# Attention with a recurrent state and a mixture of experts: the attention's preparation in an explicit order, with merged transfers and more k buffers

## The chip, the cores and the metric

The kernel runs on one core of a Trainium2 chip. The metric is the device time in microseconds of one launch. The profile is of one further execution on the same core, taken by the hardware profiler; its times are counted from the first instruction.

## The reference, cut to what matters

Attention over 4 x 8 heads of 768 tokens with 40 values each keeps a 40 x 40 state per head, which decays, loses a rank-one term and gains one at each token. Its output is the input of a router and of 8 experts, of which each token uses two.

```python
for t in range(S):
    y[:, :, t] = einsum('bhd,bhde->bhe', rt, state)
    Sa = einsum('bhde,bhe->bhd', state, at)
    state = state * wt[:, :, None, :] - einsum('bhd,bhe->bhde', Sa, bt) + einsum('bhd,bhe->bhde', vt, kt)
x = y.transpose(0, 2, 1, 3).reshape(B*S, H*D)
noisy_logits = x @ w_gate + log1p(exp(x @ w_noise)) * noise
# the two best experts of each token, weighted by a softmax of their logits:
#   out += weight * (relu(x @ w1[e]) @ w2[e])
```

## The kernel before, in words

The attention is computed in chunks of 64 tokens. A chunk of one pair of batch entries (p = 0 or 1; 16 heads) is one **step**: 24 steps, n = 0 to 23, with p alternating. Four steps (two chunks of both pairs) make a **group** g, 0 to 5. A step in `run` has these parts:

- `chain` (line 639), the only part that hands something to a later step of its pair: it multiplies the state into `W`, applies the triangular inverse `T` of its chunk twice (`pQ<-w,T`), writes `vu`, sums the new state in `pS` and scales it into `Sst` on VectorE (line 667). The `Sst` instruction is what this text counts steps by: step n ends with `Sst` number n.
- `pre` (line 602) and `blocks` for the next step, `outp` (line 669) for this step's output `xt`, which `Moe.logits` stores and feeds to the router.
- `fetchA` (line 576) and `fetchB` (line 590) load what step n+2 needs: `Vz`, `vu`, `RV`, the k stack `st_k`, and `T`.

Ahead of its steps a group needs its **preparation**, in two halves (one for each pair). `prepA` (line 486) loads `raww` and `rawba`, forms the running products of the decays with some ten VectorE instructions and two of ScalarE, packs b and a into fp16 pairs `pk`, stores these to `d_ab` in DRAM and reads them back as `st_ab` in another layout. `scoresL` (line 549) multiplies them on TensorE and stores the scores to `scr`. When both halves are there, `tsolve` (line 560) reads `scr` as `X`, inverts 32 x 32 triangles in 30 pairs of instructions, and stores `scr2`, from which `T` is fetched. The solver runs on VectorE for groups 0 and 1 and on GpSimd for groups 2 to 5 (`TPOOL`). `prepC` (line 534) loads `rawk` into the one buffer there is (`RKB=1`), scales and packs it and stores it to `d_k`, from which `st_k` is read.

The order on each engine is set by the Tile scheduler: it sorts the instructions by a priority (the order in the program, moved by `high_priority`) and by when its own model of the machine has them ready; `issue_after`, `Behind` (line 393) and `burst` add constraints. Each engine then runs its list strictly in that order, and so does the queue of SyncE (SP), which issues nearly all DMAs: an instruction that waits holds up all that stand behind it on that engine. In the loop of `run`, `prepA` of group (n+7)//4 is written ahead of the chain of step n when the remainder is 0 or 1, and `prepC` of group (n+4)//4 likewise:

```python
g,c,p,cc=idx(n); ga,qa=divmod(n+LA,4); gc,qc=divmod(n+LC,4)      # L726
if ga>1 and ga<NG and qa<2: ... prepA(ga,qa)
if 0<gc<NG and qc<2: ... prepC(gc,qc)
```

After the 24 steps `Moe.experts` runs the 8 experts with TensorE in products of three terms (lines 287 and 309); it is not touched by the change. During the steps `Moe.route` sends 2 to 8 tiles of 128 tokens at a time to `Moe.place` (line 153), which builds one-hot tiles `ohA`, `ohD` and `ohB` of two token tiles (`TW=2`) on VectorE, multiplies them on TensorE and adds the result to `tab`; `drain` works off one such call per step.

Of the kernel before, what the change touches and what calls it, by code (L numbers as in the profile page):

```python
# [8 lines left out]
F32 = mybir.dt.float32  # L9
# [9 lines left out]
CAP=832; NX=128; SLT=1024; TW=2  # L19
# [20 lines left out]
class Moe:  # L40
# [107 lines left out]
    def drain(s,n=9):  # L148
# [216 lines left out]
NS=6*CG  # L365
# [38 lines left out]
class Att:  # L404
# [81 lines left out]
    def prepA(s,p,g):  # L486
        nc=s.nc; FM=s.aps[0]; V=Behind(s.tc,nc.vector,s.tl) if g==1 else nc.vector
        sh=[120,NS,64]; W0=NS*65
        w=s.inp.tile([120,W0],F32,name="raww",bufs=2); nc.sync.dma_start(w,FM[p,g][:,:W0])
        ba=s.inp.tile([120,2*X],F32,name="rawba",bufs=BAB)  # L490
        for i in range(2): nc.sync.dma_start(ba[:,X*i:X*i+X],FM[p,g][:,W0+X*i:W0+X*i+X])
        b_,a_=ba[:,:X],ba[:,X:]
# [13 lines left out]
        s.pl=(V if g in MG else nc.gpsimd).tensor_tensor(NG_,Gx[:,:,0:64],nr[:,:,31:32].to_broadcast(sh),op=ALU.mult)  # L506
# [17 lines left out]
        for gg in range(3): nc.sync.dma_start(sv[40:120,gg],dv[:,gg])  # L524
# [9 lines left out]
    def prepC(s,G,gate=None):  # L534
        nc=s.nc; FM=s.aps[2]; p,g=G['p'],G['g']
        after=lambda i: s.tc.issue_after(gate[i].ins) if gate else ExitStack()
        kf=s.inp.tile([120,X],F32,name="rawk",bufs=RKB)
        with after(0): nc.sync.dma_start(kf,FM[p,g])
        if p==0 and g==0:
            s.mags=s.cp.tile([120,1],F32,name="mags")  # L540
            nc.vector.tensor_reduce(s.mags,kf[:,0:64],axis=AX.X,op=ALU.max)
        k_=kf.rearrange("p (c a b t)->p c a (b t)",c=CG,a=3,b=2)
        for b in range(2):
            k1=k_[:,:,:,64*b:64*b+64]; (nc.vector if g in MK else nc.gpsimd).tensor_tensor(k1,k1,G['NH'].rearrange("p (a c b) t->p b c a t",a=3,c=CG)[:,b],op=ALU.mult)
        d=G['d']=s.dr.tile([CG,2,120,384],F16,name="d_k",bufs=4)
        def out(pk):
            with after(1): s.nc.sync.dma_start(d.rearrange("c l p x->p (c l) x"),pk)
        s.pack(kf,-SC,1,CG,out)
    def scoresL(s,G,gi,scr):

        nc=s.nc
        lt=s.tmp.tile([128,CG,8,32],F32,name="lt",bufs=LTB)
        lo=s.late.tile([128,CG,8,32],F32,name="lo",bufs=LOB)
        for c in range(CG):
            pp=s.score64(G['b'][c],G['a'][c],"pp",s.PPB)
            for z,t0 in ((lt,0),(lo,32)): nc.scalar.activation(z[:,c],pp[:,:,t0:t0+32],AF.Copy,scale=-(2.0**-18))
        for i in range(4):
            s.sl=s.nc.sync.dma_start(scr[gi,i].rearrange("c h (j t)->j (c h) t",j=32),(lt,lo)[i%2][32*i:32*i+32].rearrange("p c h t->p (c h) t"))
        G['lo']=lo
    def tsolve(s,scr,eng):  # L560
        nc=s.nc
        Xt=s.tmp.tile([128,32,32],F32,name="X",bufs=2)
        s.xd=s.nc.sync.dma_start(Xt.rearrange("p a b->p (a b)"),scr.rearrange("g i c h x->(g i c h) x"))
# [75 lines left out]
    def chain(s,p,cc,o):  # L639
# [20 lines left out]
        if not last:  # L660
# [32 lines left out]
    def run(s,m,xo=None):  # L693
# [3 lines left out]
        def prepA(g,p):  # L697
            if p==0: grp[g]=[]; scr[g]=s.dr.tile([2,4,CG,8,1024],F32,name="scr")
# [19 lines left out]
        with after(s.sl.ins): fA(1)
# [26 lines left out]
LA=7; LC=4; RB=3  # L745
# [21 lines left out]
BAB=1; RKB=1  # L767
# [130 lines left out]
```

## Time and profile before

| | |
|---|---|
| median of 3 runs | 1033.28 us (1033.17 to 1034.09) |
| the profiled execution's own time | 1035.52 us |
| its span, first to last instruction | 1033.7 us |
| busy share of the span: TensorE, its weight loads, VectorE, ScalarE, GpSimd | 79%, 69%, 54%, 38%, 31% |
| mean granted TensorE clock | 0.904 |
| moved by DMA | 135.89 MB, 131 GB/s on average |
| chain of work that ended last | TensorE 53%, VectorE 21%, DMA 14% |

The profiled execution's own time is 1.8 us above its span, for what lies around the first and the last instruction. The page cuts the span in 40 slices and gives the busy share of each engine in each; the chain is followed back from the last instruction, at each step to what released it or to the instruction ahead of it on its engine. Steps are read from the starts of the 22 `Sst` instructions, from 101.69 us (step 0) to 556.1 us (step 21); the last two steps write no state. Step 3 ends at 200.5 us, step 4 at 229.6, step 7 at 280.6, step 8 at 315.2, step 11 at 369.7, step 12 at 400.5, step 16 at 465.1 and step 20 at 530.2 us; the attention's last output is written at 601.8 us.

### The profile page before, as it was taken

Reading aid. Unit: us, or ns where it says so; the run is one execution under the profiler, and the core shown is the slowest. Engines: PE = TensorE matmul, PEld = TensorE weight load, DVE = VectorE, ACT = ScalarE, POOL = GpSimd, SP = SyncE. Lnnn points to the kernel's source line nnn. Section 1 sums busy time; section 2 is a strip of 40 time slices with the busy share of each in tenths; the row PEclk is TensorE's granted clock in tenths of the full one; section 3 lists DMA queues with packets and bytes.
Section 4 is the critical chain, followed back from the end, with each engine's and each line's share of the span. In section 5 each row is a group of like instructions: output and inputs, shape, how many; then the busy total and the mean of one; then the engine's idle time right before and its main releaser. Section 6 shows DMA issues by size and latency. Waiting matters only on the chain.

```text
span 1033.7 us, 27409 instructions
## 1 busy us (share of the span) xinstructions
PE 814.5 (79%) x11706; PEld 712.2 (69%) x11706; DVE 554.3 (54%) x1198; ACT 391.0 (38%) x820; POOL 321.1 (31%) x456
## 2 busy tenths in 40 slices
PE   0114558669857876998896789999999999999994
PEld 0113446557746755877775668898989898989994
DVE  9268667944757666338554762643434444443420
ACT  2203443334633542454443432543434444443420
POOL 5000000393077039209401005316060606060312
PEclk9999986558967976998997699999999999999997
DMA  4785896593784684473486403516161616161302
GB/s 121 183 231 127 214 266 151 146 239 102 163 247 156 139 209 112 116 173 121 127 256 203 126 8 73 163 24 167 28 154 43 159 37 157 38 148 49 36 8 37
DMA packets 127111, 135.89 MB, mean 131 GB/s; under 512 B 59248, under 2 KB 106804, under 8 KB 126900
## 3 DMA queue, kind: packets, MB, share of 16 engines
q1 hardware_dynamic: 116292, 114.90, 41.5%
q0 software_dynamic: 10688, 19.14, 9.7%
q8 instruction: 94, 1.54, 0.6%
q14 instruction: 37, 0.30, 0.1%
HBM read 96.25 MB, written 41.03 MB: 133 GB/s over the span
## 4 chain that ended last, share of the span: by engine, by line
PE 53%; DVE 21%; DMA 14%; issue 4%; ACT 4%; SPq 3%; POOL 0%; POOLq 0%; DVEq 0%; ACTq 0%
PE po L309 17%; PE ph L287 15%; DMA rawk<-in_fm_dram 6%; PE psc L470 4%; PE pY L470 3%; DMA d_ab<-pk 2%; PE pW L470 2%; PE pQ L470 2%; PE pt L268 2%; DVE X L571 2%; DVE Tt L570 2%; DVE w2l L244 1%; DVE pk L460 1%; PE pst L470 1%; DVE ohB L162 1%
## 5 line engine op out<-in xcount | busy, mean ns | idle before, releaser
L311 POOL DMA_INDIRECT out_dram<-y,oi x56 | 92.3, 1648 | 236.9 <-ACT y L310 212.1
L290 DVE SCALAR_TENSOR_TENSOR hl<-ph,hh 128x256 fp32r<-128x256 f32 (+1 forms) x128 | 70.1, 554 | 120.5 <-ACT hh L288 111.3
L288 ACT ACTIVATE hh<-ph 128x320 fp32r<-128x320 f32 (+1 forms) x128 | 64.7, 518 | 147.6 <-PE ph L287 141.5
L564 POOL TENSOR_TENSOR X<-X,tri 128x1024 f32<-128x1024 f32 x4 | 9.0, 2242 | 309.2 <-DVE ak L606 179.3
L309 PE MATMUL po<-w2h,hh 128*128 128x320 f32 x384 | 75.4, 314 | 5.0 <-DVE y L304 3.9
L470 PE MATMUL psc<-RV,uT 128*64 128x128 f32 x384 | 63.0, 317 | 17.0 <-DVE P L680 15.1
L571 POOL TENSOR_TENSOR X<-X,Tt 128x30 f32<-128x30 f32 (+14 forms) x120 | 72.2, 602 | 8.7
L570 POOL TENSOR_TENSOR Tt<-X 128x30 f32<-128x30 f32 (+14 forms) x120 | 70.1, 584 | 8.4
L309 PE MATMUL po<-w2h,hl 128*128 128x320 f32 x384 | 70.8, 311 | 0.0
L287 PE MATMUL ph<-xh,w1h 128*128 128x512 f32 (+1 forms) x256 | 69.7, 355 | 1.0 <-DVE hl L290 1.0
L470 PEld LDWEIGHTS psc<-RV,uT 128*64 128x64 f32 x384 | 50.0, 160 | 27.6 <-DVE P L680 16.5
L287 PE MATMUL ph<-xh,w1l 128*128 128x512 f32 (+1 forms) x256 | 68.9, 350 | 0.0
L287 PE MATMUL ph<-xl,w1h 128*128 128x512 f32 (+1 forms) x256 | 68.6, 349 | 0.0
L252 POOL DMA_INDIRECT xr<-xd,gi x56 | 53.7, 959 | 47.6 <-issue 14.3
L309 PEld LDWEIGHTS po<-w2h,hh 128*128 128x128 f32 x384 | 61.0, 188 | 9.9 <-issue 5.0
L309 PE MATMUL po<-w2l,hh 128*128 128x320 f32 x384 | 65.7, 309 | 0.0
L470 PE MATMUL pQ<-w,T 32*32 32x40 f32 x2304 | 46.7, 224 | 23.7 <-DMA T<-scr 23.1
L680 DVE TENSOR_TENSOR P<-psc,mk 128x512 f32<-128x512 f32 x48 | 32.9, 686 | 59.3 <-PE psc L470 59.1
L470 PEld LDWEIGHTS pQ<-w,T 32*32 32x32 f32 x2304 | 39.6, 128 | 36.3 <-issue 32.1
L470 PE MATMUL psc<-RV 128*64 128x128 f32 x384 | 63.1, 317 | 0.0
L309 PEld LDWEIGHTS po<-w2h,hl 128*128 128x128 f32 x384 | 59.8, 188 | 0.5
L309 PEld LDWEIGHTS po<-w2l,hh 128*128 128x128 f32 x384 | 58.6, 188 | 0.1
(312 smaller groups left out, 1883.7 us busy)
## 6 DMA issues: line engine op xcount, KB each, us to landing
w2r<-in_w_dram SPq DMA_DIRECT2D x8, 1280.0 KB
RV<-in_rv_dram SPq DMA_DIRECT2D x48, 192.0 KB
rawba<-in_fm_dram SPq DMA_DIRECT2D x24, 360.0 KB
d_ab<-pk SPq DMA_DIRECT2D x24, 360.0 KB
st_ab<-d_ab SPq DMA_DIRECT2D x36, 240.0 KB
w1r<-in_w_dram SPq DMA_DIRECT2D x8, 1024.0 KB
raww<-in_fm_dram SPq DMA_DIRECT2D x12, 365.6 KB
st_ab<-d_ab SPq DMA_DIRECT2D x24, 180.0 KB
```

The costliest lines, as they stand in the source:

```text
L162: nc.vector.tensor_tensor(B[:,j],D[:,j].rearrange("p k (o m)->p k o m",o=1).to_broadcast([128,2,4,64]),vl[:,j].rearrange("p k (f o)->p k f ...
L252: k=t//128; nc.gpsimd.indirect_dma_start(out=X[:p,k if s.cap==CAP else 0],out_offset=None,in_=s.xd[int(w is not s.early[0])],in_offset=OFF ...
L268: for t,p in tiles(t0,n): nc.tensor.transpose(pt[:,t-t0:t-t0+p],x[:p,t//128,f0:f0+128],s.idm[:p,:p])
L287: for i,(a,b) in enumerate(mm): nc.tensor.matmul(ph[:,:n],a,b,start=i==0,stop=i==7)
L288: nc.scalar.activation(hh[:,f,:n],ph[:,:n],AF.Relu)
L290: if c.stop>c.start: nc.vector.scalar_tensor_tensor(o,ph[:,c],0.0,hh[:,f,c].bitcast(F32),op0=ALU.max,op1=ALU.subtract)
L309: s.lm=nc.tensor.matmul(po[:p],h[:,f,r],w[:,f],start=k==0,stop=k==23); k+=1
L311: st=nc.gpsimd.indirect_dma_start(out=s.out_d,out_offset=OFFS(ap=idx[:p,e,ii:ii+1],axis=0),in_=y[:p],in_offset=None,compute_op=ALU.add)
L470: def mm(s,*a,**k): return lambda: s.nc.tensor.matmul(*a,**k)
L570: eng.tensor_tensor(t,Xt[:,j:j+1,j+1:].to_broadcast([128,j,m]),Xt[:,0:j,j:j+1].to_broadcast([128,j,m]),op=ALU.mult)
L571: s.tl=eng.tensor_tensor(Xt[:,0:j,j+1:],Xt[:,0:j,j+1:],t,op=ALU.add)
L680: nc.vector.tensor_tensor(m,pp.rearrange("p i j t->p (i j) t"),s.mk.to_broadcast([128,8,64]),op=ALU.mult)
```

## The change

- In the loop, the preparation of group n//4 + 2 is tied to the steps: `prepA` of its halves in the first and the third step of four, `scoresL` in the second and the fourth (on TensorE behind the `pS` products of the same step), `prepC` in the second and the fourth too, the solver in the fourth. All of its VectorE instructions stand behind the `Sst` of the step before (`Behind`, with `aD`). So `prepC` of groups 2 to 5 runs about a group earlier than it did, and `prepA` somewhat later.
- The loads of `raww`, `rawba` and `rawk` are split off (`loadA`, `loadC`) and written a step or more ahead of their use; `rawk` has two buffers, there are four `st_k` stacks instead of three and six `d_k` in place of four.
- Merged transfers: `T` of a step comes in one DMA instead of four (the scores lie in another order in DRAM for it), `st_ab` in three instead of five. In a step's fetches `vu` and `RV` come last (`fetchR`).
- `X` of the solver has one buffer instead of two. `Moe.place` works on one token tile at a time, two calls per step.

The diff, cut to its core (`V` stands for VectorE, as in the kernel):

```diff
-CAP=832; NX=128; SLT=1024; TW=2
+CAP=832; NX=128; SLT=1024; TW=1
...
-    def prepA(s,p,g):
+    def loadA(s,p,g):
...
+        return w,ba
+    def prepA(s,p,g,raw=None,first=None):
+        nc=s.nc
+        if g==1: first=s.tl
+        V=Behind(s.tc,nc.vector,first) if first is not None else nc.vector
+        w,ba=raw or s.loadA(p,g)
...
-        for gg in range(3): nc.sync.dma_start(sv[40:120,gg],dv[:,gg])
+        nc.sync.dma_start(sv[40:120].rearrange("p g x n->p (g x n)"),dv.rearrange("p g x n->p (g x n)"))
...
+    def loadC(s,G):
+        kf=s.inp.tile([120,X],F32,name="rawk",bufs=RKB); s.nc.sync.dma_start(kf,s.aps[2][G['p'],G['g']])
+        return kf
+    def prepC(s,G,gate=None,kf=None,first=None):
...
-        Xt=s.tmp.tile([128,32,32],F32,name="X",bufs=2)
+        Xt=s.tmp.tile([128,32,32],F32,name="X",bufs=1)
...
-        for i in range(4):
-            s.nc.sync.dma_start(T[32*i:32*i+32],scr2[p,i,c].rearrange("h j x->j h x"))
+        s.nc.sync.dma_start(T,scr2[p,c].rearrange("h i j x->(i j) h x"))
...
         for n in range(N):
-            if ga>1 and ga<NG and qa<2:
-                with (after(s.sd0.ins) if n<=GA else ExitStack()): prepA(ga,qa)
-                if qa: prepT(ga)
-            if 0<gc<NG and qc<2:
-                with (after(s.sd0.ins) if n<=GC else ExitStack()): prepC(gc,qc)
+            g,c,p,cc=idx(n); w,q=divmod(n,4); gn=w+2
             with s.tc.high_priority(offset=PRIO):
                 sD=s.chain(p,cc,O[n])
+            if q%2==0 and gn<NG:
...
+                grp[gn].append(s.prepA(q//2,gn,rA.pop((gn,q//2)),aD))
+            if n<2: s.prepC(grp[1][n])
+            elif q%2==0 and gn<NG:
+                with behind(n-1): rC[gn,q//2]=s.loadC(grp[gn][q//2])
+            if q%2 and gn<NG:
+                with after(s.aP.ins): s.scoresL(grp[gn][q//2],q//2,scr[gn])
...
+                s.prepC(grp[gn][q//2],kf=rC.pop((gn,q//2)),first=aD)
+                if q==3: prepT(gn)
+            if q%2 and (gn if q==1 else gn+1)<NG:
+                z=(gn,1) if q==1 else (gn+1,0)
+                with behind(n-1): rA[z]=s.loadA(z[1],z[0])
             fB(n+2)
+            aD=s.aD
...
-                m.drain(1); m.logits(2*cc+p,xt,s.ps,("pt","pp"),(s.PT,s.PPB))
+                m.drain(2); m.logits(2*cc+p,xt,s.ps,("pt","pp"),(s.PT,s.PPB))
...
-LA=7; LC=4; RB=3
+LA=7; LC=4; RB=4
...
-BAB=1; RKB=1
+BAB=1; RKB=2
```

How the lists of the engines change is seen at three places. The first is VectorE at the end of step 8 (the `Sst` here is number 8). Before:

```order
L460 SCALAR_TENSOR_TENSOR pk<-rawba,pk 120x768
L460 SCALAR_TENSOR_TENSOR pk<-rawk,pk 120x2x384
L658 TENSOR_SCALAR vu<-pQ 64x320
L691 TENSOR_TENSOR xt<-pY,xt 128x320
L606 TENSOR_TENSOR ak<-psc,mk_127 128x512
L544 TENSOR_TENSOR rawk<-rawk,NH 120x6x64 x2
L99 SCALAR_TENSOR_TENSOR xT<-px,xT 128x384
L667 SCALAR_TENSOR_TENSOR Sst_169<-pS,gam_148 128x8x40
L625 TENSOR_TENSOR sfs<-Sst_169,sfs 128x320
```

And after the change (line 682 is `Sst`, lines 399 and 460 are the preparation, 673 `vu`, 706 `xt`, 621 `ak`):

```order
L399 SCALAR_TENSOR_TENSOR pk<-rawba,pk 120x768
L706 TENSOR_TENSOR xt<-pY,xt 128x320
L621 TENSOR_TENSOR ak<-psc,mk_127 128x512
L682 SCALAR_TENSOR_TENSOR Sst_169<-pS,gam_148 128x8x40
L399 TENSOR_TENSOR rawk<-rawk,NH 120x6x64
L99 SCALAR_TENSOR_TENSOR xT<-px,xT 128x384
L399 TENSOR_TENSOR rawk<-rawk,NH 120x6x64
L640 TENSOR_TENSOR sfs<-Sst_169,sfs 128x320
L474 COPY uT<-pu 128x512
L399 SCALAR_TENSOR_TENSOR pk<-rawk,pk 120x2x384
```

The product on `rawk`, which stood two instructions ahead of `Sst`, stands behind it.

The second is the SP queue where the solver's input `X` is loaded. Before, for group 4:

```order
L489 DMA raww<-in_fm_dram 120x780
L563 DMA X<-scr 128x1024
L95 DMA xd_839<-xt 128x320
L580 DMA Vz_172<-in_vt_dram 64x320 x2
L521 DMA d_ab<-pk 120x2x768
L491 DMA rawba<-in_fm_dram 120x768
L547 DMA d_k<-pk 120x4x384
L491 DMA rawba<-in_fm_dram 120x768
L538 DMA rawk<-in_fm_dram 120x768
L524 DMA st_ab<-d_ab 80x1536 x3
```

And after the change, for group 3 (line 526 and 528 store `d_ab`, 575 loads `X`):

```order
L526 DMA d_ab<-pk 120x2x768
L575 DMA X<-scr 128x1024
L528 DMA d_ab<-pk 120x2x768
L491 DMA rawba<-in_fm_dram 120x768
L95 DMA xd_825<-xt 128x320
L532 DMA st_ab<-d_ab 40x3x768
L602 DMA vu<-in_vt_dram 64x2x320
L491 DMA rawba<-in_fm_dram 120x768
L592 DMA Vz_173<-in_vt_dram 64x320
```

`X` now stands behind the store of the next group's first `pk`, which the next preparation on VectorE has to make first, and the load of `rawk` no longer stands here.

The third is the SP queue where `T` of group 2 is fetched, before:

```order
L95 DMA xd_839<-xt 128x320
L593 DMA T<-scr_1587 32x8x32
L581 DMA vu<-in_vt_dram 64x2x320
L593 DMA T<-scr_1587 32x8x32 x3
L580 DMA Vz_172<-in_vt_dram 64x320 x2
```

and after (line 608 fetches `T`, 531 and 532 `st_ab` of the second half of group 3, 604 `RV`):

```order
L604 DMA RV_175<-in_rv_dram 48x1024 x2
L478 DMA st_k<-d_k 40x1152
L608 DMA T<-scr_2001 128x8x32 x2
L531 DMA st_ab<-d_ab 80x4608
L532 DMA st_ab<-d_ab 40x3x768 x2
L608 DMA T<-scr_2001 128x8x32
L95 DMA xd_825<-xt 128x320
```

Four transfers per step have become one, and `st_ab` of the next half now stands behind the fetch that waits for the solver.

## Rows read from the trace of the kernel before

**Rows 1.** Busy time by stretch: the prologue, steps 1 to 4, 5 to 8, 9 to 12, 13 to 16, 17 to 20, the rest of the attention, the experts; then single steps 5, 8 and 14.
```profile
core 0: us, PE busy (x) PEld busy (x) DVE busy (x) ACT busy (x) POOL busy (x), PEclk, DMA share, GB/s
0.00:101.70 101.70, 19.33 (x395) 16.77 (x396) 68.83 (x144) 22.41 (x38) 15.24 (x63) 1.00 0.65 163
101.70:229.60 127.90, 80.19 (x1492) 66.27 (x1491) 91.27 (x167) 46.84 (x98) 30.85 (x39) 0.74 0.79 203
229.60:315.20 85.60, 65.98 (x1607) 55.02 (x1605) 46.31 (x72) 36.23 (x83) 35.99 (x61) 0.80 0.68 177
315.20:400.50 85.30, 65.95 (x1532) 54.27 (x1532) 63.56 (x145) 37.16 (x88) 35.35 (x67) 0.78 0.64 161
400.50:465.10 64.60, 58.19 (x1564) 48.31 (x1564) 23.74 (x44) 29.57 (x73) 20.18 (x35) 0.94 0.52 131
465.10:530.20 65.10, 59.07 (x1511) 49.16 (x1510) 43.83 (x116) 28.11 (x72) 35.14 (x72) 0.92 0.51 151
530.20:601.80 71.60, 55.83 (x1141) 45.70 (x1138) 41.96 (x140) 26.83 (x66) 5.76 (x12) 0.79 0.56 164
601.80:1033.70 431.90, 409.98 (x2490) 376.72 (x2488) 174.79 (x378) 163.81 (x305) 142.59 (x111) 0.99 0.35 80
...
229.60:247.40 17.80, 17.06 (x371) 14.18 (x369) 6.47 (x11) 6.41 (x16) 12.15 (x25) 0.69 0.40 120
280.60:315.20 34.60, 18.94 (x370) 15.75 (x370) 19.74 (x29) 10.33 (x23) 23.84 (x36) 0.66 0.84 232
419.90:435.60 15.70, 14.97 (x445) 12.80 (x441) 5.05 (x12) 7.96 (x21) 1.30 (x4) 1.00 0.36 97
```
**Rows 2.** The chain that ended last, in order of time: start, us, what; steps 1 to 12.
```profile
125.77 4.62 DMA rawk<-in_fm_dram
...
165.66 6.68 DMA rawk<-in_fm_dram
...
193.81 3.11 DMA scr<-X
...
209.74 8.32 DMA rawk<-in_fm_dram
...
218.12 7.05 DMA d_ab<-pk
...
227.50 5.14 DMA rawk<-in_fm_dram
...
288.82 8.33 DMA rawk<-in_fm_dram
...
306.72 6.09 DMA rawk<-in_fm_dram
...
377.24 8.07 DMA rawk<-in_fm_dram
...
397.17 5.47 DMA rawk<-in_fm_dram
```
**Rows 3.** The SP queue's timeline: start, us, the issues of `T` ahead of step 0.
```profile
85.48 6.75 SPq L593 DMA_DIRECT2D T<-scr  x12
```
**Rows 4.** GpSimd's timeline: the solver's first instruction and the store behind its last, two groups.
```profile
195.87 2.63 POOL L564 TENSOR_TENSOR X<-X,tri 128x1024 f32<-128x1024 f32 x1 [179.30 <-DVE ak L606]
...
243.04 0.83 POOL L573 DMA_DIRECT2D scr<-X  x1 [0.33 <-POOL X L571]
...
463.27 2.12 POOL L564 TENSOR_TENSOR X<-X,tri 128x1024 f32<-128x1024 f32 x1 [41.62 <-DMA X<-scr]
...
503.92 0.59 POOL L573 DMA_DIRECT2D scr<-X  x1 [0.30 <-POOL X L571]
```
**Rows 5.** Line 520 on VectorE, ns min/median/max: without a solver on GpSimd beside it, and with one.
```profile
L520 DVE TENSOR_TENSOR rawba<-rawba,NG__4022 x1: 948/948/948, 278.0 to 278.0; 120x768 f32<-120x768 f32 x1
L520 DVE TENSOR_TENSOR rawba<-rawba,NG__4427 x1: 1208/1208/1208, 301.6 to 301.6; 120x768 f32<-120x768 f32 x1
```
**Rows 6.** Groups of instructions by line and shape, up to 602 us: the adds to `tab`.
```profile
L166 DVE TENSOR_TENSOR tab<-tab,pn 128x256 f32<-128x256 f32 x11 | 4.5, 413 | 0.7 <-PE pn L165 0.7
```

More of the change, by code (lines that the diff above doesn't have):

```diff
@@ L533, in prepA @@
         return G
-    def prepC(s,G,gate=None):
-        nc=s.nc; FM=s.aps[2]; p,g=G['p'],G['g']
+    def loadC(s,G):
+        kf=s.inp.tile([120,X],F32,name="rawk",bufs=RKB); s.nc.sync.dma_start(kf,s.aps[2][G['p'],G['g']])
+        return kf
+    def prepC(s,G,gate=None,kf=None,first=None):
+        nc=s.nc; p,g=G['p'],G['g']
+        V=Behind(s.tc,nc.vector,first) if first is not None else nc.vector
         after=lambda i: s.tc.issue_after(gate[i].ins) if gate else ExitStack()
-        kf=s.inp.tile([120,X],F32,name="rawk",bufs=RKB)
-        with after(0): nc.sync.dma_start(kf,FM[p,g])
+        if kf is None:
+            with after(0): kf=s.loadC(G)
         if p==0 and g==0:
@@ L578, in fetchA, with fetchR @@
         vt=s.aps[1][p,cc]
-        o['vz']=s.Vz[n%2]; o['vu']=s.stk.tile([128,2,8,40],F32,name="vu",bufs=VUB)
+        o['vz']=s.Vz[n%2]
         for b in range(2): q=slice(64*b,64*b+64); nc.sync.dma_start(o['vz'][q,b].rearrange("p h e->p (h e)"),vt[q])
-        nc.sync.dma_start(o['vu'][0:64].rearrange("p b h e->p b (h e)"),vt.rearrange("(b s) x->s b x",b=2))
         st=s.stk.tile([120,9*128],F16,name="st_k",bufs=RB); s.stackK(st,G['d'][c])
         o['k']=s.operand(st,1,0,1,0)
+        for z in 'ab': o[z]=G[z][c]
+        o['ng']=G['ng'][:,:,c]; o['lo']=G['lo'][:,c]
+        return o
+    def fetchR(s,o,cc):
+        nc=s.nc; n,p=o['n'],o['G']['p']
+        vt=s.aps[1][p,cc]; o['vu']=s.stk.tile([128,2,8,40],F32,name="vu",bufs=VUB)
+        nc.sync.dma_start(o['vu'][0:64].rearrange("p b h e->p b (h e)"),vt.rearrange("(b s) x->s b x",b=2))
         rv=s.RV[n%2]
@@ L664, in chain @@
             s.burst(f)
-            s.burst([s.mm(Sp[64*b:64*b+40,h],o['kb'][:,b,h],vu[:,b,h],start=False,stop=True,skip_group_check=True) for h,b in HB(1)])
+            s.aP=s.burst([s.mm(Sp[64*b:64*b+40,h],o['kb'][:,b,h],vu[:,b,h],start=False,stop=True,skip_group_check=True) for h,b in HB(1)])
             gb=s.gam[p][:,0:8,cc+1:cc+2].to_broadcast([128,8,40])
-            nc.vector.scalar_tensor_tensor(s.Sst[p][:,:,0:40],Sp,IS,gb,op0=ALU.mult,op1=ALU.mult)
+            s.aD=nc.vector.scalar_tensor_tensor(s.Sst[p][:,:,0:40],Sp,IS,gb,op0=ALU.mult,op1=ALU.mult)
         return sD
@@ L697, in prepA @@
         def prepA(g,p):
-            if p==0: grp[g]=[]; scr[g]=s.dr.tile([2,4,CG,8,1024],F32,name="scr")
+            if p==0: grp[g]=[]; scr[g]=s.dr.tile([2,CG,8,4,1024],F32,name="scr")
             with s.tc.high_priority(offset=PA_):
@@ L712, in run @@
         after=s.tc.issue_after
+        behind=lambda n: ExitStack()
         prepA(0,0); prepA(0,1); pl=s.pl.ins; prepT(0); xd,tl=s.xd.ins,s.tl.ins
@@ L715, in run @@
         s.prepC(grp[0][0],gate)
-        with after(s.sl.ins): fA(0)
+        with after(s.sl.ins): fA(0); fR(0)
         s.prepC(grp[0][1],gate)
-        with after(s.sl.ins): fA(1)
+        with after(s.sl.ins): fA(1); fR(1)
         s.pre(O[0]); s.blocks(O[0]); fB(0); fB(1)
```

41 lines of the change are left out of this document (22 added, 19 removed).

## The prediction

> **What bounds the kernel now.** I read the busy time by stretch first [rows 1]. The experts, the last 431.9 us, have TensorE busy for 410.0 us at a granted clock of 0.99. The change touches nothing there, so that part stays. In the attention the same work, four steps, takes 127.9, 85.6 and 85.3 us (steps 1 to 4, 5 to 8, 9 to 12), then 64.6 and 65.1 us (13 to 16, 17 to 20). The reader is to see that no engine is full in the dear stretches: in steps 5 to 8 TensorE is busy for 66.0 of 85.6 us and VectorE for 46.3. These are waits, and the single steps show it: step 14 takes 15.7 us at clock 1.00, step 8 takes 34.6 us with VectorE busy for 19.7.
>
> The second view is the chain that ended last [rows 2]. Eight times in steps 1 to 12 it runs through a load of `rawk`, with 4.62 to 8.33 us each and 52.7 us together. One `rawk` buffer lets the next load start only when the last half is packed, and the product on it stands two instructions ahead of `Sst` in VectorE's list (the first place above), so a late load delays the state. Step 8 holds two of them, 8.33 + 6.09 = 14.4 us; without them it would be 20.2 us, still 4.5 above step 14. Once, at 218.12, the chain runs through the store of `pk` for 7.05 us.
>
> **The change part by part,** against the profiled execution's 1035.5 us.
>
> a) *`rawk` early, in two buffers, its product behind `Sst`.* The load is written more than a step ahead, which is more than the longest wait, 8.33 us. All eight waits can go: −52.7. What is late next is TensorE's own work or the other preparation, and step 8 shows how much of that there is: 4.5 us over step 14 beside two waits, 2.25 for each. If as much again stays in the place of each, eight times 2.25, 18 us, are kept: −35. I take −52.7, since the product no longer stands ahead of `Sst` whatever it waits for; ends −52.7 and −35.
>
> b) *The wait on the store of `pk`,* 7.05 us at 218.12 in step 4 [rows 2]. That half is prepared later, with the reading of `st_ab` in fewer transfers. −5; ends −7 and 0.
>
> c) *The preparation itself moves.* VectorE is busy for 91.3 us of steps 1 to 4, so taking work away there shortens them, and adding it to steps 13 to 16 (23.7 us busy of 64.6) lengthens them. The price of a group's preparation, its `rawk` waits aside: 85.6 − 17.4 = 68.2 us and 85.3 − 11.4 = 73.9 us for steps 5 to 8 and 9 to 12, against 64.6 − 2.2 = 62.4 for 13 to 16 (a wait that runs across a border is divided there). So 5.8 to 11.5 us. Steps 13 to 16 gain a group's work: +6. Steps 1 to 4 lose part of one: −4, from 0 to −11.5. Net +2; ends −6 and +12.
>
> d) *Transfers merged.* An issue of `T` takes SP 6.75/12 = 0.56 us [rows 3]. Ahead of step 0 there are eight for the first two steps, later two: 6 × 0.56 = 3.4 us. In the loop 12 issues fewer per four steps, 6.7 us of a queue which is not the bound at most steps: nothing, as long as the loads stand two steps ahead. One merged transfer could land later than four small ones. −2; ends −7 and +2.
>
> e) *TensorE's clock.* Step 5, behind a stall, took 17.8 us at a granted 0.69; step 14, behind a busy step, 15.7 us at 1.00 [rows 1]. The levels are 1.2 and 2.4 GHz, so a row between them mixes both. 2.1 us a step, for about six steps of the twelve that follow a stall, halved since the preparation leaves gaps: −6; ends −12 (all six) and 0.
>
> f) *VectorE beside GpSimd.* Now the halves of groups 3 to 5 stand wholly beside a solver. Line 520 takes 0.948 us without it and 1.208 us with it [rows 5], +0.26 us; some eleven instructions of a half make 2.9 us, for three halves more than before 8.6 us of VectorE time, of which a third is seen: +3; ends 0 and +8.
>
> The Trainium skill, page "SBUF — State Buffer", section "Who interferes with whom", speaks against this part: a VectorE instruction with two SBUF inputs and a GpSimd instruction that reads SBUF lock each other out, for the whole instruction. The row agrees that there is a loss but shows a quarter, not a whole instruction of the solver each time; by the rule taken to its end the loss of VectorE and solver would be that of the third rival below.
>
> g) *The solver starts later and SP waits for it.* `X` stands behind the store of the next half's `pk` (the second place), and `st_ab` behind the fetch of `T` (the third). In the forecast the steps hide it: +2; ends 0 and +15. More is a rival.
>
> h) *`TW=1`.* Twelve more adds to `tab` at 0.413 us [rows 6] are 5.0 us of VectorE, beside other work: +1; ends 0 and +5.
>
> i) *Loads ahead of step 0.* Two halves of `rawk`, 120 x 768 fp32 = 0.37 MB each, at the prologue's 163 GB/s [rows 1] are 2.3 us each, on a stretch that DMA fills to 0.65: +2; ends 0 and +4.5.
>
> One `X` buffer instead of two costs nothing: two solvers are a group apart, and 47.2 us (195.87 to 243.04 [rows 4]) is shorter than four steps. The fourth `st_k` stack costs SBUF alone.
>
> Sum: −52.7 − 5 + 2 − 2 − 6 + 3 + 2 + 1 + 2 = **−55.7**, so 979.8 us for a profiled execution. The median of the runs lies 2.24 us below the profiled one (1033.28 against 1035.52): **978 us**. All lower ends together give −84.7, 949 us. The upper ends together would be +11.5, but they are nine separate things; the root of the summed squares of the distances to them is 27 us: 1005.
>
> **The rivals.**
>
> R1: *the solver sets the pace.* `X` of a group is loaded in the first step of the next four, behind ten VectorE instructions of up to 1.208 us, so 12 us in. The solver takes 47.2 us with preparation beside it and 40.6 (463.27 to 503.92) without [rows 4]. Its store and `T` are two transfers, which I put at 3.1 us each, as the chain's store of `scr` at 193.81 [rows 2]: 12 + 47.2 + 6.2 = 65.4 us. Four steps would take some 68 (between 62.4 and 73.9 above). It is just in time for the fourth step to end, but `st_ab` comes behind `T` in SP's queue, and `scoresL`, which stands in the middle of the fourth step in TensorE's list, needs it: 4.6 more for that transfer (the shortest `rawk` wait), and a third of a step, 5 us, after it: 75. So 0 to 7 us, say 5 us a group, for four groups +20: **998**. Against it: a load that is issued earlier in the first step, or an `X` ahead of the tenth instruction, hides it all.
>
> R2: *another buffer takes `rawk`'s place.* `rawba` still has one buffer (`BAB=1`), and its products are now tied behind `Sst`, ahead of the next. If half of the 52.7 us returns, some 25: **1003**. Against it: no row of the chain in steps 1 to 12 names `rawba`.
>
> R3, the slower side: *the solver and the preparation slow each other, and SP's queue carries it to every engine.* If the solver lengthens as line 520 does, by 1.208/0.948 = 1.27, its 47.2 us become 60, `T` lands at 12 + 60 + 6 = 78 us, `st_ab` and the rest of the step make 88: 20 us over 68, in the three groups that have a preparation beside the solver, +60 in all, so −55.7 + 60 = +4: **1037**. Place: `T` at SP's head, with `st_ab` and the loads of the next steps behind, and TensorE at `scoresL`. It turns the sign from 56/3 = 19 us a group, that is if the solver, from 12 us on, takes over 59 us. Against it: the 47.2 us have a preparation beside them already.
>
> R4: *nothing changes,* since SP or DMA bounds the dear steps (share 0.84 in step 8) and not the order: 1033. Against it: steps 1 to 4 have 0.79 and steps 5 to 8 only 0.68 on average, and the waited-for load is one transfer.
>
> **How the numbers follow.** The forecast 0.65, R1 0.18, R2 0.06, R3 0.08, R4 0.03. The likeliest is the sum, 978. The lower end of the range is all terms' lower ends, 949, with some 5% below it, taken as 948. The upper end is 1005 for the forecast's own terms, and R1 and R2 lie within it but with ends of their own, some 10 us further; 1015 leaves out R3, R4 and a few per cent of the rest. A difference of 0.2%, 2 us, is about what can be told from no change. Faster: 0.65 + 0.18 + 0.06 = 0.89; same 0.03 (R4); slower 0.08 (R3).
>
> **What would show it.** In the profile of the changed kernel: a) no load of `rawk` in the chain from step 1 on, and step 4 ending near 203 us instead of 229.6 (229.6 less the four waits of steps 1 to 4, 21.7 us by the border, and b); c) four steps of 62 to 74 us everywhere, with steps 13 to 16 dearer than 64.6; e) a clock near 0.9 instead of 0.74 to 0.80 in steps 1 to 12; f) line 520's work at 1.2 us rather than 0.95; the attention's last output near 546 us. R1 would show as `T` or `scr` in the chain at the fourth step of each group, R2 as `rawba` or `pk` in `rawk`'s place, R3 as four steps of over 85 us with a solver of over 59. A chain through VectorE's own busy time in steps 5 to 16, or a prologue that ends later than 106 us, would make the forecast wrong in a way that I have not priced.

## The result, and the profile after

The changed kernel takes 1044.3 us (median of 4 runs, 1038.0 to 1050.0) against 1033.55 us before: 1.0107 times as long, 95% interval 1.0058 to 1.0157. Twelve more runs of it on another chip gave 1.0066 [1.0029, 1.0103]. It is slower, by some 7 to 11 us. The forecast was 978 us. The profiled execution is the fastest of the first four, 1038.03 us with a span of 1036.3 us, only 2.6 us above that of before; so its trace shows where time was won and where it was lost again, more than how much was lost in all.

The busy time by stretch of the changed kernel, the same parts of the program as [rows 1], and then single steps (4, 6, 10 and 14):

```profile
core 0: us, PE busy (x) PEld busy (x) DVE busy (x) ACT busy (x) POOL busy (x), PEclk, DMA share, GB/s
0.00:102.20 102.20, 17.86 (x387) 15.80 (x388) 67.78 (x141) 22.29 (x38) 15.24 (x63) 1.00 0.65 163
102.20:210.90 108.70, 74.44 (x1498) 62.14 (x1497) 77.59 (x153) 43.04 (x93) 0.00 (x0) 0.84 0.79 197
210.90:285.00 74.10, 62.70 (x1560) 52.82 (x1562) 46.51 (x69) 35.56 (x84) 40.80 (x63) 0.86 0.72 175
285.00:375.00 90.00, 70.00 (x1597) 57.53 (x1597) 68.21 (x149) 37.69 (x90) 43.77 (x72) 0.79 0.77 189
375.00:454.70 79.70, 65.53 (x1552) 55.09 (x1549) 38.03 (x61) 32.29 (x77) 40.45 (x63) 0.81 0.59 143
454.70:522.70 68.00, 58.30 (x1539) 48.97 (x1539) 42.93 (x121) 27.86 (x72) 37.81 (x72) 0.95 0.61 170
522.70:604.50 81.80, 58.94 (x1085) 47.42 (x1079) 43.27 (x142) 26.93 (x66) 5.76 (x12) 0.69 0.44 129
604.50:1036.30 431.80, 412.69 (x2522) 381.50 (x2520) 177.14 (x380) 165.32 (x305) 145.28 (x111) 0.98 0.34 80
...
195.85:210.91 15.06, 14.02 (x403) 11.55 (x404) 13.97 (x22) 10.71 (x25) 0.00 (x0) 1.00 0.60 135
228.09:252.56 24.47, 20.29 (x422) 17.37 (x423) 17.11 (x21) 11.00 (x25) 22.43 (x27) 0.69 0.56 142
315.86:341.85 25.99, 20.75 (x405) 16.74 (x406) 21.91 (x31) 10.46 (x23) 23.71 (x29) 0.62 0.45 110
393.64:418.78 25.14, 20.97 (x422) 17.84 (x421) 16.99 (x22) 10.93 (x25) 23.02 (x28) 0.66 0.14 39
```

Steps 1 to 8 gained, 127.9 + 85.6 us down to 108.7 + 74.1: 30.7 us. Steps 9 to 20 and the attention's end gave it back: 85.3 to 90.0, 64.6 to 79.7, 65.1 to 68.0, 71.6 to 81.8. The experts are as before. By single step (from `Sst` to `Sst`, us), with three of the experiments told below:

| step | before | changed | T behind `st_ab` | prep late | split |
|---|---|---|---|---|---|
| 3 | 26.0 | 17.9 | 17.7 | 18.1 | 18.8 |
| 4 | 29.1 | 15.1 | 15.1 | 21.9 | 15.1 |
| 8 | 34.6 | 19.3 | 16.1 | 18.2 | 25.2 |
| 12 | 30.8 | 17.4 | 18.2 | 17.9 | 24.2 |
| 2 | 34.0 | 38.8 | 38.4 | 37.5 | 37.5 |
| 6 | 18.0 | 24.5 | 23.8 | 19.5 | 19.5 |
| 7 | 15.2 | 13.1 | 14.0 | 46.5 | 16.1 |
| 9 | 19.8 | 30.9 | 27.1 | 26.2 | 21.3 |
| 10 | 18.3 | 26.0 | 25.7 | 25.3 | 18.0 |
| 14 | 15.6 | 25.1 | 25.2 | 20.6 | 18.3 |
| 16 | 12.2 | 21.5 | 13.3 | 13.5 | 28.1 |
| 20 | 14.8 | 19.9 | 19.3 | 15.2 | 21.2 |
| 21 | 25.9 | 30.8 | 30.5 | 30.9 | 21.6 |

Steps 4, 8 and 12, which held 36.3 us of `rawk`'s waits and the 7.05 us of the store of `pk` [rows 2], lost 14.0 + 15.3 + 13.4 = 42.7 us. Step 3, where the chain ran through the store of a solver (193.81 in [rows 2]) and no load of `rawk`, lost 8.1. No load of `rawk` is left in the chain behind step 0. In steps 1 and 2, which held 11.3 us of these waits, nothing was won: 72.9 us became 75.8, and the chain runs through the loads of `rawba` instead. Steps 2, 6, 9, 10, 14, 16, 20 and 21 took 58.9 us more. The chain that ended last (start, us) in steps 1 and 2, 6, and 9:

```profile
117.84 4.86 DMA rawba<-in_fm_dram
144.26 7.79 DMA rawba<-in_fm_dram
...
240.66 2.16 DVE pk L399 x2
242.82 0.61 DVE P L695
...
291.08 3.54 DMA d_ab<-pk
295.59 0.96 DVE pk L399
```

The question is what the other longer steps are. Two views give two theories.

**Theory B, a block on VectorE.** VectorE's timeline in step 4 and in step 6 (start, us, instruction; in brackets the idle time ahead of it):

```profile
195.85 0.49 DVE L682 SCALAR_TENSOR_TENSOR Sst<-pS,gam 128x320 f32<-128x320 f32 x1 [2.04 <-PE pd L471]
...
203.73 0.17 DVE L399 TENSOR_TENSOR nge<-Gx,raww 120x12 f32<-120x12 f32 x1
203.82 0.95 DVE L399 TENSOR_TENSOR rawba<-rawba,NH 120x768 f32<-120x768 f32 x1
204.69 0.68 DVE L695 TENSOR_TENSOR P<-psc,mk 128x512 f32<-128x512 f32 x1
...
228.09 0.49 DVE L682 SCALAR_TENSOR_TENSOR Sst<-pS,gam 128x320 f32<-128x320 f32 x1 [3.04 <-PE pd L471]
...
237.29 0.62 DVE L399 TENSOR_TENSOR nge<-Gx,raww 120x12 f32<-120x12 f32 x1
237.84 0.95 DVE L399 TENSOR_TENSOR rawba<-rawba,NH 120x768 f32<-120x768 f32 x1
238.71 1.36 DVE L399 TENSOR_TENSOR rawba<-rawba,NG__2980 120x768 f32<-120x768 f32 x1
...
240.58 2.23 DVE L399 SCALAR_TENSOR_TENSOR pk<-rawba,pk 120x768 f16<-120x768 f32 x2
242.74 0.68 DVE L695 TENSOR_TENSOR P<-psc,mk 128x512 f32<-128x512 f32 x1
```

In step 4 the first `P`, for which TensorE waits, starts 8.8 us behind `Sst`, in the middle of the preparation; in step 6 the whole block up to both `pk` stands ahead of it, and a solver runs beside, so it starts 14.7 us behind `Sst`. The chain goes the same way: from both `pk` at 240.66 to `P` at 242.82. The granted clock is 0.69 in step 6 against 1.00 in step 4, and TensorE's busy time 20.3 against 14.0 us for about as many matmuls.

**Theory Q, the SP queue.** SP's timeline in steps 13 to 15, where group 4's solver ends and group 5's second half waits for its scores:

```profile
408.31 0.34 SPq L528 DMA_DIRECT2D d_ab<-pk  x1
428.42 1.01 SPq L608 DMA_DIRECT2D T<-scr  x2
...
436.11 0.30 SPq L531 DMA_DIRECT2D st_ab<-d_ab  x1
436.46 1.68 SPq L532 DMA_DIRECT2D st_ab<-d_ab  x2
```

SP stands still for 19.8 us at the fetch of `T`, until the solver has stored it; `st_ab`, whose data had been on their way since 408, goes out at 436. What follows is the chain that ended last (start, us):

```profile
437.35 7.58 DMA st_ab<-d_ab
445.86 5.21 DMA T<-scr
452.04 3.69 DMA scr<-lo
455.88 5.70 DMA X<-scr
461.72 2.13 POOL X L576
...
503.23 6.72 DMA scr<-X
509.97 2.77 DMA T<-scr
```

The solver of group 5 starts at 461.7 us; in the kernel before it started at 463.3 [rows 4]. The steps up to 12 had gained 25.5 us (step 12 ended at 375.0 instead of 400.5), and this solver is 1.6 us earlier. Those of groups 2, 3 and 4 start 20.0, 9.5 and 1.2 us later than before (215.9, 298.2 and 379.3 instead of 195.9, 288.7 and 378.1). The queue stood in that order before as well:

```profile
424.96 4.69 SPq L593 DMA_DIRECT2D T<-scr  x8
...
434.22 2.76 SPq L524 DMA_DIRECT2D st_ab<-d_ab  x3
```

### The profile page after: what moved, and what is told of

The parts are those of the page before. It is cut to its first block, busy times and chain, and to the rows that moved or that the text cites. A ratio compares the mean times of both kernels' runs of the same rounds, so it can differ in the third digit from the quotient of the medians.

```text
span 1036.3 us, 27316 instructions
## 1 busy us (share of the span) xinstructions
PE 820.5 (79%) x11706; PEld 721.3 (70%) x11706; DVE 561.5 (54%) x1210; ACT 391.0 (38%) x820; POOL 329.1 (32%) x456
## 4 chain that ended last, share of the span: by engine, by line
PE 56%; DVE 15%; DMA 13%; issue 5%; POOL 4%; SPq 3%; ACT 3%; POOLq 0%; ACTq 0%; DVEq 0%
PE ph L287 18%; PE po L309 17%; PE psc L470 4%; PE pY L470 3%; DMA d_ab<-pk 3%; DMA st_ab<-d_ab 2%; PE pt L268 2%; PE pQ L470 2%; POOL X L583 2%; DMA T<-scr 2%; PE pS L470 2%; POOL Tt L582 2%; DMA d_k<-pk 1%; DVE Gx L399 1%; DMA rawba<-in_fm_dram 1%
## 5 line engine op out<-in xcount | busy, mean ns | idle before, releaser
L583 POOL TENSOR_TENSOR X<-X,Tt 128x30 f32<-128x30 f32 (+14 forms) x120 | 76.3, 636 | 8.8
L470 PE MATMUL psc<-RV,uT 128*64 128x128 f32 x384 | 67.5, 333 | 9.1 <-DVE P L695 8.1
L470 PE MATMUL psc<-RV 128*64 128x128 f32 x384 | 67.5, 333 | 0.0
L470 PEld LDWEIGHTS psc<-RV,uT 128*64 128x64 f32 x384 | 53.7, 170 | 16.2 <-DVE P L695 9.5
L470 PEld LDWEIGHTS <-st_ab 120*64 120x64 f16 (+1 forms) x928 | 28.1, 124 | 48.2 <-issue 29.7
```

The costliest lines, as they stand in the source:

```text
L470: def mm(s,*a,**k): return lambda: s.nc.tensor.matmul(*a,**k)
```

## The experiments

All ratios are to the kernel before, run beside on the same chip (its median lay between 1029 and 1041 us on the chips used), with 95% intervals. What is said of an experiment against the changed kernel is the difference of two such ratios, and its interval is some 6 us to either side. The changed kernel, run once more as it is, is the mark: 

> The changed kernel itself, unaltered, beside the next three on one chip, so that their differences to it need no detour over other chips. Every theory: 0.5 to 1.5% above the kernel before, as measured at first.

 Measured: 1.0066 [1.0029, 1.0103]; its trace has the same long steps (6, 9, 10, 14, 16: 25.3, 31.2, 25.3, 25.4, 23.6 us).

### Whose wait it is: solver, queue, block

**Half a solver.**

```diff
-        for j in range(1,31):
+        for j in range(1,31,2 if eng is nc.gpsimd else 1):
```

> The changed kernel, but the GpSimd solver (groups 2 to 5) works only every second of its 30 pairs of instructions, so that it inverts nothing and takes about half of its 41 to 47 us. Theory Q (queue: the fetch of T waits for the solver at the head of SP's queue, st_ab of the next half waits behind it, and with it scoresL, X and the next solver): the holds of SP of 10.7 us before 264.0 and 19.8 us before 428.4 vanish, the wait for T in step 20 too, and the time falls by 20 to 30 us, to 1015 to 1025. Theory B (block: the preparation stands as one block on VectorE right behind Sst, ahead of P and vu of the same step): steps 6, 10 and 14 stay at 24 to 26 us, only step 20 gains its 5 to 8 us: 1035 to 1040.

Measured: 0.9866 [0.9821, 0.9910], 20 us below the changed kernel. Step 16 fell to 13.5 us; 6, 10 and 14 only to 21.5, 22.2 and 22.7. The sum is what Q expects, but it isn't the queue's alone: steps 6, 10 and 14 give 9.2 us of it, step 16 gives 8.0. B's steps stay long without a waited-for solver. GpSimd's timeline of groups 3 and 4, changed kernel first, then with half a solver:

```profile
298.23 2.12 POOL L576 TENSOR_TENSOR X<-X,tri 128x1024 f32<-128x1024 f32 x1 [36.58 <-DMA X<-scr]
379.25 2.12 POOL L576 TENSOR_TENSOR X<-X,tri 128x1024 f32<-128x1024 f32 x1 [32.96 <-DMA X<-scr]
...
298.24 2.12 POOL L576 TENSOR_TENSOR X<-X,tri 128x1024 f32<-128x1024 f32 x1 [55.25 <-DMA X<-scr]
377.76 2.12 POOL L576 TENSOR_TENSOR X<-X,tri 128x1024 f32<-128x1024 f32 x1 [56.07 <-DMA X<-scr]
```

These two solvers don't start earlier, although the solver ahead of each is 20 to 25 us shorter; only that of group 5 does, at 450.4 instead of 461.7. So up to group 4 it isn't the solver's length that sets when the next one starts.

**`T` behind `st_ab`.**

```diff
-            fB(n+2)
+            with (after(s.sd0.ins) if q>1 and gn<NG else ExitStack()): fB(n+2)
```

> The changed kernel with one constraint on SP's order: the fetches of T in the third and fourth step of a group stand behind st_ab of the next half instead of ahead of it; nothing else moves. Q: st_ab lands without waiting for the solver, scores and X of groups 4 and 5 start up to 15 us earlier, step 20 no longer waits for T: 10 to 20 us less, 1025 to 1035. B: no change beyond 5 us, since steps 6, 10 and 14 keep their block.

Measured: 0.9973 [0.9930, 1.0015], 10 to 14 us below the changed kernel. Step 16 has lost its 8.2 us (table), and GpSimd's timeline has the last solver 12.9 us earlier than the 461.72 above:

```profile
448.80 2.12 POOL L576 TENSOR_TENSOR X<-X,tri 128x1024 f32<-128x1024 f32 x1 [28.53 <-DMA X<-scr]
```

The order of `T` and the three `st_ab` on SP is worth that. Steps 6, 10 and 14 are as they were.

**Prep late.** The second half's preparation (`PA` is `prepA`, `LC_` the load of `rawk`) is written behind `outp`:

```diff
...
             s.outp(O[n],sD,xt); xt=xt[:,0:DM]
+            if q==2 and gn<NG: PA(); LC_()
...
```

> The changed kernel with the second half's preparation (prepA and the load of rawk in the third step of a group) written behind outp of that step, still tied to the same Sst. By the order on VectorE this splits the block of steps 6 and 14 (the first P of the step now stands ahead of the product on NG, where it stood behind both pk), leaves that of step 10 whole, and makes one in step 4, where there was none. B: steps 6 and 14 fall from 24.5 and 25.1 us to 16 to 19, step 10 stays at 26, step 4 rises from 15.1 to 18 to 21, in sum 8 to 12 us less than the changed kernel: 1032 to 1037. Q: steps 6 and 14 depend on SP and the solver and stay within 2 us; no change in the time.

Measured: 1.0122 [1.0061, 1.0184], no gain, but each step moved the way that B says: 6 and 14 fell by 5.0 and 4.5 us (to 19.5 and 20.6, a little above the 16 to 19 expected), 10 stayed, 4 rose by 6.8 with the block that it now holds, and its clock fell from 1.00 to 0.84. The windows of steps 4 and 7, and ScalarE's timeline in step 7:

```profile
196.20:218.10 21.90, 16.49 (x409) 14.25 (x405) 13.92 (x22) 10.56 (x24) 0.00 (x0) 0.84 0.66 157
252.00:298.60 46.60, 19.91 (x382) 16.68 (x383) 7.55 (x13) 7.23 (x17) 19.06 (x36) 0.57 0.48 123
...
282.19 0.84 ACT L459 ACTIVATE pk<-rawk 120x768 f16<-120x768 f32 x1 [27.32 <-DMA d_ab<-pk]
```

Step 7 took it all back, by another way than `st_ab`: `pk` comes later, SP is held by `T` until 276.41, so the store of `pk` goes out only at 277.98. ScalarE waits 27.32 us for that store with the next `pk`, and TensorE waits 22.8 us for an instruction that stands behind it on ScalarE. This is Q at its largest.

**Both edits.** 

> The last edit and, with it, T's fetches behind st_ab of the next half. If B and Q are two separate causes, the gains add: 8 to 12 us for B and the 14 us that the second constraint gave by itself: 20 to 26 us less than the changed kernel, 1018 to 1025. If both are the same wait seen from two ends, no more than 14 us: 1030 or above.

 Measured: 1.0038 [0.9994, 1.0082]. Step 7 is back at 13.5 us, and step 8, the first that needs the `T` of group 2, takes 38.1: that group's solver now starts at 230 us instead of 216. The gains don't add.

**No tie to `Sst`** (`first=None` for both preparations). 

> The changed kernel without the tie of the preparation to the Sst of the step before (the scheduler places the VectorE instructions of both halves by its own priorities, between the steps' own instructions). B: steps 6, 10 and 14 fall from 24 to 26 us to 16 to 19, together 20 to 27 us less: 1017 to 1025. Q: the pace is set by solver and SP; at most 5 us less, or more time where the preparation comes later. The forecast's first term (rawk's waits come from the product ahead of Sst): waits on preparation ahead of Sst come back, so slower than the changed kernel by 10 us or more.

 Measured: 1.0205 [1.0135, 1.0274]. The scheduler put the preparation ahead of loads that weren't there: `rawba` is in the chain for 51 us, step 7 takes 44.2. Steps 6 and 14 fell to 15.0 and 13.3 us, below the 16 to 19 that B expected, step 10 only to 22.8, and the sum is B's miss: what came out is the 10 us or more on the slower side that the forecast's first term expected, though the waits are for `rawba` and none for `rawk`. The tie itself is not the loss.

### Parts of the change alone

**A second `rawk` buffer in the kernel before** (`RKB=2`, one `X` to make room). 

> The kernel before with two buffers for rawk and, to make room, one for X; nothing else. If the eight waits for rawk were due to its one buffer and worth their length, as the forecast's first term has it, this alone gives 35 to 53 us: 980 to 1000. If they only cover what is late next (st_ab, the solver, the preparation on VectorE), it gives under 15 us: above 1018.

 Measured: 1.0269 [1.0209, 1.0329], slower by 28 us, which neither expectation had. Five waits for `rawk` stay, and with one `X` SP's list has `st_ab` of group 2 behind the store of the solver that runs on VectorE:

```profile
192.05 0.34 SPq L573 DMA_DIRECT2D scr<-X  x1
192.49 0.83 SPq L525 DMA_DIRECT2D st_ab<-d_ab  x1
```

In the kernel before that `st_ab` went out at 181.04, ahead of the store at 193.81. Group 2's solver starts at 215 us instead of 195.9. The forecast had put the one `X` at nothing; whether it or the second `rawk` buffer costs the 28 us, this run doesn't separate.

**One `rawk` buffer in the changed kernel.** 

> The changed kernel with one rawk buffer again, its load and its product where the change put them. If the second buffer is what took the waits out of steps 3, 4, 8 and 12, they come back: 30 to 50 us more than the changed kernel. If it is the place of the product, behind Sst and not ahead of it, the load may come late without holding the state: at most 10 us more.

 Measured: 1.0015 [0.9979, 1.0051], 5 us below the changed kernel on the same chip. The second buffer gains nothing: one load of `rawk` is back in the chain, 7.09 us in step 2. What took the others away is the place of load and product; since none came back either where the product was untied, the load's earlier place is the likelier of the two, which no run separates.

**`TW=1` alone in the kernel before.** 

> The kernel before with one-hot tiles of one token tile (two calls a step); nothing else. The forecast's term h: +1 us, 5 at most, so 1033 to 1039. Rival: the smaller tiles cost what steps 20 and 21 of the changed kernel lose, 10 us: 1043.

 Measured: 1.0183 [1.0117, 1.0248], 19 us slower, far above both. Where TensorE waited ahead of the one-hot products (line 165), with `TW=1`:

```profile
its engine sat idle before it (us, times) until:
  DVE ohB L162: 8.6, 9
  issue: 6.5, 15
  DVE ohA L160: 5.8, 5
```

With `TW=2` the first and the last are 2.0 us (2 times) and 1.4 (2): the wait for the tiles rose by 11 us. In steps 13 to 21 the granted clock fell from 0.92 to 0.81 and TensorE's busy time rose from 136.6 to 150.4 us.

**`TW=2` in the changed kernel** (`RB=3` for room). 

> The changed kernel with one-hot tiles of two token tiles and one call a step again, as before; to make room there are three st_k stacks. Theory H (small one-hot tiles make TensorE wait for VectorE twice as often at a product that stands in order in its list, and its clock falls with it): as the same edit alone cost the kernel before 1.8%, 10 to 20 us less than the changed kernel, most of it in steps 13 to 21. The forecast's term h: 1 us, at most 5 less.

 Measured: 1.0024 [0.9987, 1.0060], 4 us below the changed kernel, which is term h's size and not theory H's. The 19 us of the kernel before are not there to be regained; that other waits lie over the same steps here would explain it and is not shown.

**`T` in four transfers.**

```diff
-        s.nc.sync.dma_start(T,scr2[p,c].rearrange("h i j x->(i j) h x"))
+        [s.nc.sync.dma_start(T[32*i:32*i+32],scr2[p,c][:,i].rearrange("h j x->j h x")) for i in range(4)]
```

> The changed kernel with T of a step in four transfers again instead of one. The forecast's term d: the merge is worth 2 us, 7 at most: 1044 to 1051. A rival, that one transfer lands later than four and makes SP's hold longer: 3 to 8 us less, 1036 to 1041.

Measured: 1.0012 [0.9978, 1.0045], 5 us or more below the changed kernel: the merge gains nothing.

### What beats both, and what it leaves

**`TW=2` and `T` behind `st_ab`.** 

> The same and, with it, T's fetches behind st_ab on SP. If H and Q are separate, their gains add: 24 to 34 us less than the changed kernel, which is 1.3 to 2.3% below the kernel before. If both shorten the same wait before steps 16 to 21, no more than 14 to 20 us less.

 Measured: 0.9833 [0.9780, 0.9886]: 1.7% faster than before, 24 us below the changed kernel. The two gains, 4 and 10 to 14 us, add; the excess is within the intervals.

**The same, `T` in four.** 

> The version with two-tile one-hots and T behind st_ab, and T in four transfers per step as before. Term d (the merge is worth 2 us, 7 at most): 2 to 7 us slower than without this edit, ratio to the kernel before 0.985 to 0.990. Rival M (a T in one transfer delays what stands behind it): 5 to 10 us faster, 0.974 to 0.979.

 Measured: 0.9820 [0.9765, 0.9876], no difference to tell. These two are the fastest versions that compute everything.

**The same as the first, preparation split.** 

> The version with two-tile one-hots and T behind st_ab, in which the second half's preparation of groups 3 to 5 is split: the products on b and a and both pk stand behind the first P of the step (they land partly behind the next Sst). B: steps 6, 10 and 14 fall from 23 to 25 us to 16 to 19 each; if nothing behind them is late, 15 to 20 us less, ratio 0.963 to 0.969. Q: the later pk makes st_ab, scores and solver later; what steps 6, 10 and 14 gain, steps 7, 11, 15 and the first steps of the next group lose, so no change, 0.98 to 0.99, or more time.

 Measured: 0.9865 [0.9817, 0.9914]. Steps 6, 10 and 14 take 19.5, 18.0 and 18.3 us (table; 23.5, 23.6 and 23.5 with `TW=2` alone), with the first `P` 9.4 to 11.4 us behind `Sst` instead of 14.2 to 14.4. B is right about what they cost, and Q about the sum: steps 8 and 12 lose it, where the chain runs through the store of the solver and `T`, and so does 16, through that store and `st_ab`.

**Half a solver in it.** 

> The version with two-tile one-hots and T behind st_ab, with every second pair of instructions of the GpSimd solver left out (no inverse). If the solver still sets the end of steps 8, 16 and 20 there, 10 us or more less, ratio under 0.974; if, with st_ab ahead of T, only the block on VectorE and the steps' own work are left, within 6 us: 0.977 to 0.989.

 Measured: 0.9726 [0.9670, 0.9781], 11 us less: the solver is still waited for.

**Solver a step earlier,** both halves in neighbouring steps, in the changed kernel and in the better one:

```diff
-            if q%2==0 and gn<NG:
+            if q<2 and gn<NG:
...
-            if q%2 and gn<NG:
-                with after(s.aP.ins): s.scoresL(grp[gn][q//2],q//2,scr[gn])
+            if q in (1,2) and gn<NG:
+                with after(s.aP.ins): s.scoresL(grp[gn][q-1],q-1,scr[gn])
+                if q==2: prepT(gn)
```

> The changed kernel with one edit: the two halves' preparation stands in the first and second step of four (it was first and third), scoresL in the second and third, and so the solver goes off a step earlier. Theory L (the change spread a group's halves over more steps, so the solver starts a step later against the step that needs its T: 215.8 us instead of 195.9 for group 2, and every later one follows at its own 81 to 82 us): the solver of group 2 starts 12 to 20 us earlier, T is no longer waited for, 15 to 25 us less than the changed kernel, ratio to the kernel before 0.98 to 0.99. B: the same blocks on VectorE, in neighbouring steps, cost at least as much: no gain, 1.00 to 1.02.

Measured: 1.0277 [1.0233, 1.0320]. 

> The same on the version with two-tile one-hots and T behind st_ab. L: what half a solver gained there, some 11 us, is gained here by an earlier start: ratio 0.965 to 0.975 instead of 0.983. B: 0.98 or above.

 Measured: 0.9986 [0.9956, 1.0017]. Theory L falls. The first solver does start 16 us earlier, but the last one doesn't:

```profile
199.49 2.13 POOL L576 TENSOR_TENSOR X<-X,tri 128x1024 f32<-128x1024 f32 x1 [182.90 <-DMA X<-scr]
...
466.05 2.29 POOL L576 TENSOR_TENSOR X<-X,tri 128x1024 f32<-128x1024 f32 x1 [33.57 <-DMA X<-scr]
```

Two blocks in a row (steps 4 and 5: 24.0 and 23.7 us) and `st_ab`, three times in the chain with 7.0 to 8.2 us, lie behind that.

## Why the prediction was wrong, point by point

- **Term a, −52.7, held in steps 4, 8 and 12:** their 36.3 us of `rawk`'s waits are gone, and with them **term b**, the 7.05 us of the store of `pk` (the chain names that store in steps 1, 2 and 9 instead). It did not hold in steps 1 and 2, where loads of `rawba` (12.65 us) stand in the place of 11.3 us of `rawk`. Its reason held in one half: the product's and the load's place did it, not the second buffer (one buffer in the changed kernel is no slower).
- **The step that failed is the one from the terms to the sum:** that a wait gone from the chain shortens the kernel by its length while the preparation's new place (term c) and SP's new order (term g, "in the forecast the steps hide it") cost 2 us each. The steps did not hide them. The preparation stands as a block on VectorE ahead of `P`, and beside the steps runs a second path, from `pk` over `st_ab`, scores, `X`, solver and `T` to the step that needs `T`. For the last group it has no slack: its solver starts at 463.3 us before and at 461.7 after, and moving `st_ab` ahead of `T` alone makes it 12.9 us earlier. That this path lay hidden under the `rawk` waits before is argued from these starts and was not tried on the kernel before.
- **Term g, +2 (0 to +15),** was mis-sized: the order on SP alone costs 10 to 14 us, shown by moving `T` behind `st_ab`, and half a solver takes away 20.
- **Term c, +2,** looked for the price of the preparation in windows and not in the order on VectorE. The block ahead of `P` costs 4 to 7 us a step in steps 6, 10 and 14, shown by splitting it and by making one in step 4. The prediction had named a chain through VectorE's own busy time in steps 5 to 16 as a sign of an unpriced error, and that is what came: in steps 6, 10 and 14 the chain lies on the block for 9.8, 7.4 and 10.3 us. **Term f** was a part of it: the block's twelve instructions take 13.0 us in step 6 beside the solver and 9.9 in step 4 without, 3.1 a half against the 2.9 worked out; but they stand ahead of `P`, on the path, and not a third of them.
- **Term e, −6, had the wrong sign in the later steps.** The granted clock rose in steps 1 to 8 (0.74 and 0.80 to 0.84 and 0.86), and fell in 13 to 16 and in the attention's end (0.94 and 0.79 to 0.81 and 0.69); over the span it is 0.904 in both.
- **Term h, +1, is 4 us** in this kernel (the interval of the difference is wider than that). **Term d, −2, is none** or a loss. **Term i, +2, is 0.5:** step 0 ends at 102.20 us instead of 101.69.
- **The rivals.** R3 had the sign and the place, `T` at SP's head with `st_ab` and the scores behind it; its price was wrong, since the solver, from its start to its store, takes 45.0, 47.4, 44.8 and 41.5 us, against 47.2, 45.3, 43.0 and 40.7 before, and never over 59. That its 1037 us lies near the measured time is luck. R1 had the path, but ended its sum at the first step of the next four: it gave 65.4 us to `T` and 75 to the end of the step, while from one solver's start to the next it takes 82.4, 81.0 and 82.5 us in the changed kernel. Nor does the solver set that pace as R1 has it: half a solver leaves the first two distances at 80.7 and 79.5 us. R2 came true in steps 1 and 2, by the two loads of `rawba`. The chances were wrong most of all: 0.08 and 0.18 for a path with no slack, while the text itself had found it "just in time".
- **What stays open:** the distance from the best version (0.982) to the forecast (0.946). Every edit of the block that shortened a long step lengthened another, and half a solver is worth 11 us of it; what of the rest is VectorE's, and what the latency of the path, wasn't settled. Of the 58.9 us, the 21.1 of steps 9, 20 and 21 aren't explained by an experiment. In step 9 the trace has the wait of prep late's step 7 on a smaller scale: ScalarE waits 7.9 us with `pk` for the store of an older one, which SP issues at 291.08 only, and TensorE 5.9 us behind it; no edit moved that store alone. Step 20, in which the chain waits for `T` at 509.97, still takes 21.5 us with half a solver, and step 21 takes 28.4. A preparation with less work on VectorE wasn't tried.

## What to carry to other kernels

When a wait is taken off the path, look for the path that ran beside it and ask when its last piece starts: here twelve steps were 25.5 us ahead and the last solver 1.6. On a queue that runs strictly in order, a fetch that waits for a long computation belongs behind every transfer that the next computation needs. An explicit order that puts a long preparation behind one instruction of the chain puts it ahead of the next one, so count what stands between the two.

## What the runs showed of the hardware

Most of VectorE's instructions in the block take longer beside the solver on GpSimd, and by about the same time whatever their size: `nge` (120 x 12) 0.17 us alone and 0.62 beside it, `rawba` x `NG` (120 x 768) 0.95 and 1.36 us. Not all do: `rawba` x `NH`, as large, takes 0.95 us in both steps. The same addition for a 64th of the elements speaks for a wait and not for a slower rate. That fits the Trainium skill, page "SBUF — State Buffer", section "Who interferes with whom", where contention for the ports that VectorE shares with GpSimd is an exclusive lock. Over the twelve instructions of a block the loss is 3.1 us, 0.26 each, which is the figure of [rows 5]. The solver loses beside the block too; the same instruction beside it and behind it:

```profile
233.89 1.23 POOL L583 TENSOR_TENSOR X<-X,Tt 128x234 f32<-128x234 f32 x1
245.51 0.65 POOL L583 TENSOR_TENSOR X<-X,Tt 128x234 f32<-128x234 f32 x1
```

TensorE's clock goes with such waits: in steps 6, 10 and 14 VectorE's `P` comes 6 to 7 us later behind `Sst` than in step 4, and the steps are 9 to 11 us longer than step 4, with the granted clock at 0.62 to 0.69, between its two levels, instead of 1.00, and 6 to 7 us more of TensorE's busy time.
